# Top-32 attention and MoE on one core: both exponentials of a slot in a row, and the normalising of its weights in the same turn

## The chip, the core and the metric

One NeuronCore of a Trainium2 chip runs the whole program. The metric is the device time of one execution in microseconds (us): the median of three runs. A profiled execution has a time of its own and a span, from its first to its last instruction.

## What is computed

```python
scores = scale * np.matmul(q, k.transpose(0, 1, 3, 2))        # 8 x 8 heads, 576 x 576, head width 64
kth = np.partition(scores, -top_k, axis=-1)[..., -top_k:-top_k + 1]   # top_k = 32
scores = np.where(scores >= kth, scores, -1000000000.0)
attn = np.exp(scores - np.max(scores, axis=-1, keepdims=True))
attn = attn / (np.sum(attn, axis=-1, keepdims=True) + 1e-09)
x = np.matmul(attn, v)              # then reshaped to 4608 tokens x 512
out = ((x @ w1) * (x @ w2) @ w3) @ w_out
```

All is float32. `w3 @ w_out` is formed once at the start.

## The kernel before

The attention is cut into 144 slots, 18 for each of 8 batches: 128 query rows of the two heads of a pair (a = 0, 1), so that a slot's scores are two blocks of 128x576. One **turn** of the loop at L480 (counter `p`) works at four slots at once: it takes the scores of slot i = p+1 out of PSUM, searches the 32 largest of slot p, masks and exponentiates slot j = p-1, and normalises, transposes and multiplies with V slot m = p-2. Who does what:

- **PE** (matmul): scores `st` (L178), nine transposes into `tp` and `ro` (`turn`, L284), 20 products with V into `ro` (`values`, L303), and between them three *fillers* (`fill`, L442) of 11, 11 and 10 matmuls of the MoE of the batch before: 32 a turn. 288 of them make half a batch, so a half takes nine turns.
- **DVE**: the search (`top32_steps`, L212): four max/min over thirds of the row into `w`, then four rounds of MAX8, with match-replace behind the first three. The last MAX8 pair goes over the whole row, 128x576. Also `take_low` (`xf`, reads the values from `ro`), the reciprocal (`invert`, L277), and a product `whole` for the MoE.
- **ACT**: the mask's Relu and the exponentials (`exps`, L270, with a sum over the row as a by-product), the copies out of PSUM (`s` from `st`, `pts` from `tp`, `pr` from `ro`, `xf`), and for the MoE `asb`, `osb` and the cast `g`.
- **POOL** (GpSimd): `edge` (the two bounds of a slot, from its top 32), the mask's subtractions into `pab`, `over`, the addition to the sums (`enlarge`, L274), the two multiplications that normalise `pab` (L280), and for the MoE `g` minus its rounding.

Nothing here is reordered by a scheduler: the class `InOrder` (L37) keeps each engine's instructions in the order in which the Python code issues them, so an engine that waits holds all that stands behind it. All those instructions carry line L49 in the profile, and are told apart by their tiles. In a filler, the evictions that the MoE has put off come first, for example `take_b` (L340): `whole` on DVE, the cast `g` on ACT, the subtraction `g` on POOL.

Buffers that tie the engines: `tp` and the two `st` of a turn share two PSUM buffers (L178, L284: pool `ps_a`), so a turn's `tp` overwrites the first `st` of the turn before, once ACT and DVE have read it. `ro` has one buffer (`ps_v`): its transpose waits for `take_low` of the slot before.

For the first 17 turns or so there is no MoE. In its place `warm` (L465, five times a turn) decodes 40 pieces of the weights in steps on ACT (`t`, `y`), DVE (`z`, `y`) and POOL (`y`, `wo`, `wl`), and PE folds `w3 @ w_out` (`pf`, copied out by ACT and DVE as `wf`).

Of the kernel before, what the change touches and what calls it, by code (L numbers as in the profile page):

```python
# [14 lines left out]
ALU = mybir.AluOpType  # L15
# [42 lines left out]
def attn_moe(ctx: ExitStack, tc: tile.TileContext, q, k, v, w1, w2, w3, w_out, out, flag, general):  # L58
# [12 lines left out]
    pe, act, dve, pool, sp = nc.tensor, nc.scalar, nc.vector, nc.gpsimd, nc.sync  # L71
# [26 lines left out]
    if not general:  # L98
        pe, act, dve, pool, sp = (InOrder(tc, e) for e in (pe, act, dve, pool, sp))
# [78 lines left out]
    def scores(pairs, t):  # L178

        out = []
        for lo, hi in PARTS:
            st = ps_a.tile([128, 2, 512], F32, tag="a", name="st")
            for a in range(2):
                cut = slice(lo + 64, hi + 64) if a == 0 else slice(lo, hi)
                if t == 4:
                    qt, kt, _ = pairs[a]  # L190
                    for i, p in enumerate(HEADS):
                        pe.matmul(st[HEADS[i ^ a], a, : hi - lo], qt[p, 512:], kt[p, cut], start=True, stop=True)
                else:
                    (qt, kt, _), p = pairs[0], HEADS[a]
                    pe.matmul(st[:, a, : hi - lo], qt[p, t * 128 : (t + 1) * 128], kt[p, cut], start=True, stop=True)
            out.append(st)
        return out

    def new_s():
        return att_p.tile([128, 2, S], F32, tag="s", name="s", bufs=3)  # L200
# [5 lines left out]
    def behind(ins, first, why):  # L206
        tc.add_manual_dep(
            ins.ins, first.ins.name, mybir.DependencyInfo(mybir.DependencyClass.Sync, mybir.DependencyReason.DATA),
            reason=why,
        )  # L210

    def top32_steps(s, st, taken, slot):  # L212

        w = att_p.tile([128, 2, S], F32, tag="w", name="w", bufs=1)
        top = tops[slot % len(tops)]  # L220
        one, two, three = slice(0, NG), slice(NG, 2 * NG), slice(2 * NG, S)
        in_two, in_three = st[0][:, :, NG : 2 * NG], st[1][:, :, :NG]
        dve.tensor_tensor(w[:, :, three], s[:, :, one], in_two, op=ALU.max)
        yield dve.tensor_tensor(w[:, :, two], s[:, :, one], in_two, op=ALU.min)
        ins = dve.tensor_tensor(w[:, :, one], w[:, :, three], in_three, op=ALU.max)
        behind(ins, taken, "one engine at a time reads a bank of the scores")
        dve.tensor_tensor(w[:, :, three], w[:, :, three], in_three, op=ALU.min)
        yield
        for i in range(4):
            cut = slice(i * 8, (i + 1) * 8)  # L230
            for a in range(2):
                dve.max(top[:, a, cut], w[:, a, one] if i < 3 else w[:, a, :])
            if i < 3:
                for a in range(2):
                    dve.match_replace(w[:, a, one], top[:, a, cut], w[:, a, one], NEG)
                yield

    def edges_of(slot):
        top = tops[slot % len(tops)]
        edge = small.tile([128, 2, 2], F32, tag="edge", name="edge")  # L240
        pool.tensor_tensor(edge, top[:, :, 0:32:31], coef, op=ALU.mult)
        return edge

    def compare(slot):
        top = tops[slot % len(tops)]
        pool.tensor_tensor(over[:, 2 * slot : 2 * slot + 2], top[:, :, 31], top[:, :, 23], op=ALU.subtract)
# [15 lines left out]
    def new_weights():  # L262
        return att_p.tile([128, 2, S], F32, tag="pab", name="pab"), small.tile([128, 2], F32, tag="sums", name="sums")

    def mask(s, edge, pab, a):

        act.activation(pab[:, a, :], s[:, a, :], AF.Relu, bias=edge[:, a, 1:2], scale=-STEEP)
        pool.tensor_tensor(pab[:, a, :], s[:, a, :], pab[:, a, :], op=ALU.subtract)

    def exps(edge, pab, sums, a):  # L270
        p = pab[:, a, :]
        act.activation(p, p, AF.Exp, bias=edge[:, a, 0:1], scale=SCALE, accum_out=sums[:, a : a + 1])

    def enlarge(sums):  # L274
        pool.tensor_scalar(sums, sums, 1e-9, None, op0=ALU.add)

    def invert(sums):  # L277
        dve.reciprocal(sums, sums)

    def normalise(pab, sums):  # L280
        for a in range(2):
            pool.tensor_scalar(pab[:, a, :], pab[:, a, :], sums[:, a : a + 1], 1.0, op0=ALU.mult, op1=ALU.mult)
# [13 lines left out]
    def take_turned(tp, ro):  # L296
        pts = att_p.tile([128, 2, 512], F32, tag="pts", name="pts", bufs=1)
        act.copy(pts, tp)
        pr = att_p.tile([128, 128], F32, tag="pr", name="pr")
        act.copy(pr, ro[:, :128])  # L300
        return pts, pr
# [21 lines left out]
    def take_high(to, ov):  # L323
        for x, cols, n in to:
            act.copy(x[:, 0, cols], ov[:, n])

    def take_low(to, ov):
        for x, cols, n in to:
            dve.tensor_tensor(x[:, 1, cols], ov[:, n], x[:, 0, cols].bitcast(F32), op=ALU.subtract)
# [69 lines left out]
    if general:  # L399
# [3 lines left out]
        with tc.For_i(0, B, 1) as b:  # L403
            seen = small.tile([1, 1], I32, tag="seen", name="seen", bufs=1)
            nc.sync.dma_start(seen, flag[ds(b + 1, 1), :])
            with tc.If(nc.values_load(seen, min_val=0, max_val=1) > 0):
                kv, xs = {}, {}
                for hps, t in SLOTS:
# [3 lines left out]
                    s, st = new_s(), scores([kv[hp] for hp in hps], t)  # L412
# [20 lines left out]
    kv, ss, sts, edges, pabs, xts, lows = {}, {}, {}, {}, {}, {}, {}  # L433
# [4 lines left out]
    def evict():  # L438
        while put_off:
            put_off.pop(0)()  # L440

    def fill(n):  # L442
        evict()
        while queue and n:
            if next(queue[0], "end") == "end":
                queue.pop(0)
            else:
                n -= 1
# [4 lines left out]
    def fetch_pair(u):  # L453
        if u < B * NHP:
            kv[u] = load_pair(u // NHP, u % NHP)
# [4 lines left out]
    def prefetch(n):  # L460
        while waiting and len(fetched) < n:
            src, step = waiting.pop(0)
            fetched.append((fetch(src), step))

    def warm():  # L465

        if p < 0:
            return
        turns.append(p)
        if fetched and len(turns) % 2:  # L470
            z, step = fetched.pop(0)
            going.append(step(z))
        going[:] = [unit for unit in going if next(unit, "end") != "end"]
        prefetch(3)
# [4 lines left out]
    n_slots = len(slots)  # L479
    for p in range(-1, n_slots + 3):  # L480
        i, j, m = p + 1, p - 1, p - 2
        if i < n_slots and slots[i][1] == 3:
            fetch_pair(slots[i][0][0] + 2)
        finder = top32_steps(ss[p], *sts.pop(p), p) if 0 <= p < n_slots else iter(())
        next(finder, None)
        if 0 <= m < n_slots:
            enlarge(pabs[m][1])
            invert(pabs[m][1])
        if 0 <= j < n_slots:
            edges[j] = edges_of(j)  # L490
        if 0 <= m < n_slots:
            normalise(*pabs[m])
        next(finder, None)
        if m - 1 in lows:
            take_low(*lows.pop(m - 1))
            if m % NS == 0:
                b = m // NS - 1
                queue.append(moe_steps(b, [xts.pop(b * NHP + hp) for hp in range(NHP)], put_off.append))
        warm()
        if 0 <= j < n_slots:  # L500
            pabs[j] = new_weights()
            for a in range(2):
                mask(ss[j], edges[j], pabs[j][0], a)
            compare(j)
        fill(SHARE[0])
        next(finder, None)
        if 0 <= m < n_slots:
            tp, ro = turn(pabs[m][0])
            pts, pr = take_turned(tp, ro)
        warm()  # L510
        if 0 <= j < n_slots:
            exps(edges[j], *pabs[j], 0)
        fill(SHARE[1])
        next(finder, None)
        warm()
        if i < n_slots:
            st = scores(pairs_of(i), slots[i][1])
            ss[i] = new_s()
            take_scores(ss[i], st, 0)
        if 0 <= j < n_slots:  # L520
            exps(edges[j], *pabs[j], 1)
        if i < n_slots:
            sts[i] = st, take_scores(ss[i], st, 1)
        if 0 <= m < n_slots:
            us, t = slots[m]
            for u in us:
                if u not in xts:
                    xts[u] = new_x()
            ov = values([kv[u][2] for u in us], t, pts, pr, ro)
            lows[m] = places([xts[u] for u in us], t), ov  # L530
            take_high(*lows[m])
        next(finder, None)
        warm()
        fill(SHARE[2])
        for _ in finder:
            pass
        if 0 <= m < n_slots:
            del ss[m], pabs[m], edges[m]
        warm()
# [61 lines left out]
```

## Time and profile before

| | |
|---|---|
| time, median of 3 runs | 1324.32 us (1323.19 to 1325.38) |
| profiled execution: its time | 1324.6 us |
| its span | 1322.8 us |
| mean granted TensorE clock | 0.977 |
| busy: PE / DVE / ACT / POOL | 1225.7 / 1144.5 / 949.1 / 863.2 us |

The page gives each engine's busy time as a share of the span. The kernel has three stretches: the start with the decoding (to about 228 us), 126 turns with the MoE of the batch before (to about 1235 us), and the MoE of the last batch, on PE nearly alone. Shares over the whole span mix these, so the stretches are read apart.

### The profile page before, as it was taken

Reading aid. Unit: us, or ns where it says so; the run is one execution under the profiler, and the core shown is the slowest. Engines: PE = TensorE matmul, PEld = TensorE weight load, DVE = VectorE, ACT = ScalarE, POOL = GpSimd, SP = SyncE. Lnnn points to the kernel's source line nnn. Section 1 sums busy time; section 2 is a strip of 40 time slices with the busy share of each in tenths; the row PEclk is TensorE's granted clock in tenths of the full one; section 3 lists DMA queues with packets and bytes.
Section 4 is the critical chain, followed back from the end, with each engine's and each line's share of the span. In section 5 each row is a group of like instructions: output and inputs, shape, how many; then the busy total and the mean of one; then the engine's idle time right before and its main releaser. Section 6 shows DMA issues by size and latency. Waiting matters only on the chain.

```text
span 1322.8 us, 30010 instructions
## 1 busy us (share of the span) xinstructions
PE 1225.7 (93%) x10513; PEld 1045.4 (79%) x10513; DVE 1144.5 (87%) x3980; ACT 949.1 (72%) x2025; POOL 863.2 (65%) x1201
## 2 busy tenths in 40 slices
PE   3688846999999999999999999999999999999996
PEld 1444424888888889888888888888988888888996
DVE  7989889999999999999999999999999999999100
ACT  5776687777777787777777777777777777777311
POOL 4767697776767676766667676767677676667210
PEclk9899877999999999999999999999999999999998
DMA  6343320001020201110010101010111001000000
GB/s 232 115 139 112 126 94 23 28 22 59 17 64 12 68 13 49 31 50 20 27 53 21 59 17 63 13 50 30 49 31 48 22 21 59 17 15 2 19 19 21
DMA packets 28981, 63.89 MB, mean 48 GB/s; under 512 B 3220, under 2 KB 11412, under 8 KB 28820
## 3 DMA queue, kind: packets, MB, share of 16 engines
q1 hardware_dynamic: 28820, 61.88, 14.4%
q8 instruction: 85, 1.39, 0.5%
q14 instruction: 76, 0.62, 0.2%
HBM read 52.43 MB, written 9.44 MB: 47 GB/s over the span
## 4 chain that ended last, share of the span: by engine, by line
PE 75%; POOL 10%; ACT 7%; issue 4%; DVE 3%; DMA 0%; SPq 0%; POOLq 0%; ACTq 0%; DVEq 0%
PE ab L49 26%; PE eo L49 16%; PE st L49 11%; PE ro L49 11%; PE tp L49 9%; POOL pab L49 5%; PE pf L49 3%; ACT pab L49 2%; ACT s L49 2%; POOL g L49 2%; DVE w L49 1%; POOL y L49 1%; DVE top L49 1%; ACT g L49 1%; ACT xf L49 1%
## 5 line engine op out<-in xcount | busy, mean ns | idle before, releaser
L49 DVE MAX8 top<-w 128x8 f32<-128x192 f32 (+1 forms) x1152 | 469.1, 451 | 0.0
L49 PE MATMUL ab<-xf,wh 128*128 128x288 f32 x2048 | 430.6, 300 | 0.0
L49 POOL TENSOR_TENSOR pab<-s,pab 128x576 f32<-128x576 f32 x288 | 404.6, 1429 | 4.7 <-ACT pab L49 4.7
L49 PEld LDWEIGHTS ab<-xf,wh 128*128 128x128 f32 x2048 | 331.3, 189 | 8.3 <-issue 7.4
L49 PE MATMUL ab<-xf,wl 128*128 128x288 f32 x1024 | 307.4, 300 | 0.0
L49 DVE MATCH_REPLACE8 w<-top,w 128x192 f32<-128x192 f32 x864 | 291.2, 347 | 0.0
L49 POOL TENSOR_SCALAR pab<-pab,sums 128x576 f32<-128x576 f32 x288 | 212.5, 753 | 78.4 <-DVE sums L49 57.9
L49 ACT COPY pts<-tp 128x1024 f32<-128x1024 f32 x144 | 146.2, 1015 | 152.7 <-PE tp L49 151.0
L49 ACT ACTIVATE pab<-s,edge 128x576 f32<-128x576 f32 x288 | 209.6, 782 | 54.6 <-POOL edge L49 52.4
L49 PE MATMUL eo<-g,wf 128*128 128x288 f32 x1536 | 228.4, 300 | 0.0
L49 ACT ACTIVATE pab<-pab,edge 128x576 f32<-128x576 f32 x288 | 225.2, 782 | 1.6 <-POOL pab L49 1.3
L49 PE MATMUL tp<-ident,pab 128*128 128x128 f32 x1152 | 166.1, 284 | 64.8 <-POOL pab L49 53.6
L49 ACT COPY s<-st 128x768 f32<-128x768 f32 (+1 forms) x288 | 181.9, 632 | 48.2 <-PE st L49 39.8
L49 PEld LDWEIGHTS eo<-g,wf 128*128 128x128 f32 x1536 | 208.1, 188 | 7.2 <-issue 7.2
L49 PEld LDWEIGHTS tp<-ident,pab 128*128 128x128 f32 x1152 | 134.6, 144 | 88.6 <-POOL pab L49 87.2
L49 PE MATMUL st<-kt,qt 64*128 64x192 f32 (+3 forms) x1280 | 188.8, 445 | 16.0 <-ACT pab L49 7.4
L49 PEld LDWEIGHTS ab<-xf,wl 128*128 128x128 f32 x1024 | 193.6, 189 | 4.8 <-issue 4.8
L49 POOL TENSOR_TENSOR g<-whole,g 128x288 fp32r<-128x288 f32 x128 | 103.0, 805 | 139.7 <-ACT g L49 139.7
L49 DVE TENSOR_TENSOR w<-s,st 128x384 f32<-128x384 f32 x288 | 146.7, 551 | 29.4 <-ACT s L49 18.3
L49 PEld LDWEIGHTS st<-kt,qt 64*128 64x128 f32 (+1 forms) x1280 | 100.2, 182 | 88.9 <-issue 34.8
L49 DVE TENSOR_TENSOR w<-w,st 128x384 f32<-128x384 f32 x288 | 157.7, 548 | 5.0
L49 PE MATMUL ro<-pts,vt 128*64 128x128 f32 (+1 forms) x2560 | 161.5, 269 | 0.0
(46 smaller groups left out, 1128.5 us busy)
## 6 DMA issues: line engine op xcount, KB each, us to landing
z<-in_w SPq DMA_DIRECT2D x32, 512.0 KB, 3.6
vt<-in_v SPq DMA_DIRECT2D x32, 352.0 KB, 3.5
kt<-in_k SPq DMA_DIRECT2D x32, 320.0 KB, 3.3
qt<-in_q SPq DMA_DIRECT2D x32, 288.0 KB, 2.9
out_t<-osb SPq DMA_DIRECT2D x64, 144.0 KB, 1.7
z<-in_wo SPq DMA_DIRECT2D x8, 512.0 KB, 5.0
flag<-missed SPq DMA_DIRECT2D x1, 0.0 KB
seen<-flag SPq DMA_DIRECT2D x1, 0.0 KB
```

The source lines that it names most:

```text
L49: ins = fn(*args, **kw)
```

## The change

The second exponential of slot j is issued directly behind the first, ahead of the two copies of the next scores. The addition to the sums, the reciprocal and the normalising, until now done at the start of the next turn, follow in the same turn: the addition behind `take_high`, the reciprocal and the multiplications behind the third round of the search and ahead of its last MAX8 pair. The first `yield` of the search is gone, as nothing is put in between there now.

```diff
@@ top32_steps
         dve.tensor_tensor(w[:, :, three], s[:, :, one], in_two, op=ALU.max)
-        yield dve.tensor_tensor(w[:, :, two], s[:, :, one], in_two, op=ALU.min)
+        dve.tensor_tensor(w[:, :, two], s[:, :, one], in_two, op=ALU.min)
         ins = dve.tensor_tensor(w[:, :, one], w[:, :, three], in_three, op=ALU.max)
@@ the loop over turns
-        next(finder, None)
-        if 0 <= m < n_slots:
-            enlarge(pabs[m][1])
-            invert(pabs[m][1])
         if 0 <= j < n_slots:
             edges[j] = edges_of(j)
-        if 0 <= m < n_slots:
-            normalise(*pabs[m])
         next(finder, None)
...
             exps(edges[j], *pabs[j], 0)
+            exps(edges[j], *pabs[j], 1)
         fill(SHARE[1])
         next(finder, None)
         warm()
...
             take_scores(ss[i], st, 0)
-        if 0 <= j < n_slots:
-            exps(edges[j], *pabs[j], 1)
-        if i < n_slots:
             sts[i] = st, take_scores(ss[i], st, 1)
...
             take_high(*lows[m])
+        if 0 <= j < n_slots:
+            enlarge(pabs[j][1])
         next(finder, None)
         warm()
+        if 0 <= j < n_slots:
+            invert(pabs[j][1])
+            normalise(*pabs[j])
         fill(SHARE[2])
```

What it moves shows at three places. First ACT, in a turn with the MoE in which a cast `g` comes in the second filler (`pab<-s,edge` is the Relu, `pab,sums<-pab,edge` an exponential, `s<-st` a copy of scores). Before:

```order
L49 ACTIVATE pab<-s,edge 128x576 x2
L49 COPY asb<-ab 128x288
L49 COPY pts<-tp 128x1024
L49 COPY pr<-ro 128x128
L49 ACTIVATE pab,sums<-pab,edge 128x576
L49 CAST g<-whole 128x288
L49 COPY s<-st 128x2x384
L49 ACTIVATE pab,sums<-pab,edge 128x576
L49 COPY s<-st 128x2x192
L49 CAST xf<-ro 128x128
```

and now:

```order
L49 ACTIVATE pab<-s,edge 128x576 x2
L49 COPY asb<-ab 128x288
L49 COPY pts<-tp 128x1024
L49 COPY pr<-ro 128x128
L49 ACTIVATE pab,sums<-pab,edge 128x576 x2
L49 CAST g<-whole 128x288
L49 COPY s<-st 128x2x384
L49 COPY s<-st 128x2x192
L49 CAST xf<-ro 128x128
```

The cast `g` of the second filler now stands behind both exponentials, and the copies of the scores behind all three. Second POOL, over the same turn and the end of the one before, in which `g` came in the first and the third filler (`sums<-sums` is the addition, `pab<-pab,sums` the normalising, `pab<-s,pab` the mask). Before:

```order
L49 TENSOR_TENSOR over<-top_97 128x2
L49 TENSOR_TENSOR g<-whole,g 128x288 x2
L49 TENSOR_SCALAR sums<-sums 128x2
L49 TENSOR_TENSOR edge<-top_95,coef 128x4
L49 TENSOR_SCALAR pab<-pab,sums 128x576 x2
L49 TENSOR_TENSOR pab<-s,pab 128x576 x2
L49 TENSOR_TENSOR over<-top_95 128x2
L49 TENSOR_TENSOR g<-whole,g 128x288
L49 TENSOR_SCALAR sums<-sums 128x2
```

and now:

```order
L49 TENSOR_TENSOR g<-whole,g 128x288
L49 TENSOR_SCALAR sums<-sums 128x2
L49 TENSOR_SCALAR pab<-pab,sums 128x576 x2
L49 TENSOR_TENSOR g<-whole,g 128x288
L49 TENSOR_TENSOR edge<-top_95,coef 128x4
L49 TENSOR_TENSOR pab<-s,pab 128x576 x2
L49 TENSOR_TENSOR over<-top_95 128x2
L49 TENSOR_TENSOR g<-whole,g 128x288
L49 TENSOR_SCALAR sums<-sums 128x2
L49 TENSOR_SCALAR pab<-pab,sums 128x576 x2
```

Before, the `g` of the third filler stood ahead of the addition to the sums; now it stands behind the normalising and ahead of the next `edge`, and it is the `g` of the second filler that stands between a slot's mask and the addition to the same slot's sums. Third ACT at the start, in a turn with decoding (`t<-z` and `y<-z` are decoding steps). Before:

```order
L49 COPY pr<-ro 128x128
L49 ACTIVATE t<-z 128x512
L49 ACTIVATE y<-z 128x512
L49 ACTIVATE pab,sums<-pab,edge 128x576
L49 COPY s<-st 128x2x384
L49 ACTIVATE pab,sums<-pab,edge 128x576
L49 COPY s<-st 128x2x192
L49 CAST xf<-ro 128x128
L49 ACTIVATE t<-z 128x512
```

and now:

```order
L49 COPY pr<-ro 128x128
L49 ACTIVATE t<-z 128x512
L49 ACTIVATE y<-z 128x512
L49 ACTIVATE pab,sums<-pab,edge 128x576 x2
L49 COPY s<-st 128x2x384
L49 COPY s<-st 128x2x192
L49 CAST xf<-ro 128x128
L49 ACTIVATE t<-z 128x512
```

The second exponential no longer stands between a copy that waits for PE's scores and the decoding step behind it.

## Rows read from the trace of the kernel before

**Rows 1.** Stretches: length, busy us (instructions) of PE PEld DVE ACT POOL, PEclk, DMA
```profile
14.00:228.00 214.00, 144.95 (x837) 83.27 (x838) 191.34 (x580) 152.88 (x301) 157.34 (x185) 0.88 0.33 109
309.00:453.00 144.00, 142.90 (x1300) 126.24 (x1298) 135.68 (x487) 110.90 (x242) 99.10 (x142) 1.00 0.12 37
```

**Rows 2.** Waits, 309 to 453 us: who on whom, us in total, times, longest
```profile
DVE sums L49 <- POOL sums L49: 3.3, 4, 0.9
```

**Rows 3.** Timeline of DVE, one turn without MoE work, and a start nine turns later
```profile
717.75 1.02 DVE L49 TENSOR_TENSOR w<-s,st 128x384 f32<-128x384 f32 x2
...
719.80 0.28 DVE L49 TENSOR_TENSOR xf<-ro,xf 128x128 fp32r<-128x128 f32 x1
...
723.51 1.42 DVE L49 MAX8 top<-w 128x8 f32<-128x576 f32 x2
725.03 0.56 DVE L49 TENSOR_TENSOR w<-s,st 128x384 f32<-128x384 f32 x1
...
789.82 0.55 DVE L49 TENSOR_TENSOR w<-s,st 128x384 f32<-128x384 f32 x1
```

**Rows 4.** Timeline of PE: the transposes of two turns in a row
```profile
784.64 1.03 PE L49 MATMUL tp<-ident,pab 128*128 128x128 f32 x8
...
792.49 0.38 PE L49 MATMUL tp<-ident,pab 128*128 128x128 f32 x2
```

**Rows 5.** Timeline of a turn behind a third-filler g: POOL, DVE, ACT
```profile
749.93 0.80 POOL L49 TENSOR_TENSOR g<-whole,g 128x288 fp32r<-128x288 f32 x1 [3.01 <-ACT g L49]
750.80 0.21 POOL L49 TENSOR_SCALAR sums<-sums 128x2 f32<-128x2 f32 x1
751.10 0.20 POOL L49 TENSOR_TENSOR edge<-top,coef 128x4 f32<-128x4 f32 x1
751.31 1.47 POOL L49 TENSOR_SCALAR pab<-pab,sums 128x576 f32<-128x576 f32 x2
752.75 2.81 POOL L49 TENSOR_TENSOR pab<-s,pab 128x576 f32<-128x576 f32 x2
...
751.05 0.17 DVE L49 RECIPROCAL sums<-sums 128x2 f32<-128x2 f32 x1 [0.81 <-POOL sums L49]
...
753.57 0.45 DVE L49 TENSOR_TENSOR whole<-ab,asb 128x288 f32<-128x288 f32 x1
753.93 0.61 DVE L49 MAX8 top<-w 128x8 f32<-128x192 f32 x2
...
751.33 1.44 ACT L49 ACTIVATE pab<-s,edge 128x576 f32<-128x576 f32 x2 [1.47 <-POOL edge L49]
...
753.59 1.02 ACT L49 COPY pts<-tp 128x1024 f32<-128x1024 f32 x1 [0.54 <-PE tp L49]
...
754.65 0.79 ACT L49 ACTIVATE pab<-pab,edge 128x576 f32<-128x576 f32 x1
...
755.42 0.43 ACT L49 CAST g<-whole 128x288 fp32r<-128x288 f32 x1
...
755.93 0.80 POOL L49 TENSOR_TENSOR g<-whole,g 128x288 fp32r<-128x288 f32 x1 [0.22 <-ACT g L49]
```

**Rows 6.** Waits of DVE at the start, 14 to 228 us
```profile
DVE z L49 <- ACT y L49: 14.4, 14, 3.0
DVE wf L49 <- ACT wf L49: 3.5, 2, 2.5
```

**Rows 7.** Timeline of one turn at the start
```profile
136.28 1.01 DVE L49 TENSOR_TENSOR w<-s,st 128x384 f32<-128x384 f32 x2
...
138.27 1.97 PE L49 MATMUL tp<-ident,pab 128*128 128x128 f32 x8 [3.70 <-POOL pab L49]
...
146.38 0.80 ACT L49 COPY s<-st 128x768 f32<-128x768 f32 x1 [2.99 <-PE st L49]
147.07 0.78 ACT L49 ACTIVATE pab<-pab,edge 128x576 f32<-128x576 f32 x1
...
149.63 0.69 DVE L49 TENSOR_SCALAR z<-t 128x512 int32<-128x512 int32 x1 [3.05 <-ACT y L49]
```

## The prediction, before the changed kernel was run

> **What bounds the kernel now.** I read the stretches first, then the waits, then single turns of the timeline. Of the profiled execution's 1324.6 us (0.3 above the median of 1324.32), the start and the 126 turns with MoE work matter here; the MoE of the last batch runs behind the last turn and has nothing to do with the exponentials. In the turns with MoE PE is busy 142.9 of 144 us and DVE 135.7 of 144 [rows 1]: two engines within a few per cent of full, so neither share says what a wait is worth. The timeline does. Nine turns, half a batch of MoE, take 789.82 - 717.75 = 72.07 us on DVE [rows 3]. PE, where nothing holds it, repeats its turn in 792.49 - 784.64 = 7.85 us [rows 4], nine times 70.65. So 1.42 us of every nine turns are lost to waits of PE; there are fourteen such nines, and **20 us is all that these turns can give**. DVE alone would need 725.03 - 717.75 = 7.28 us for a turn without MoE work [rows 3], and 0.36 more for each `whole` (753.57 to the next start at 753.93) [rows 5]; a nine has eight of them, so DVE has little more room than PE while the `g` come.
>
> Where the 1.42 goes is seen in rows 5. A `g` of the third filler is cast late on ACT, behind the copies of the scores, and its subtraction stands on POOL ahead of the addition to the sums (749.93, 750.80); the reciprocal waits 0.81 for that, the normalising starts only at 751.31, and the transposes behind it. That happens in two turns of nine: four waits, 3.3 us in a batch [rows 2].
>
> **The change, part by part, in the turns with MoE.** No instruction is added or dropped; the reciprocal's 0.08 (its share of DVE's pipelined issue) only moves. No DMA moves, and neither SP's nor POOL's queue is passed by one. What moves are waits.
>
> *Gone*: the normalising (1.44, from 751.31 to 752.75) no longer stands between a slot's bounds and its mask on POOL [rows 5], and a third-filler `g` no longer stands ahead of the sums. The transposes no longer wait for the normalising, which now ends in the turn before.
>
> *What is late next*: two things. First the reciprocal, now ahead of the last MAX8 pair. I count from the start of DVE's turn. DVE comes to it at 723.51 - 717.75 - 0.08 = 5.68, or 6.04 with a `whole` before it, and the next turn starts 1.60 after it (0.08, and 1.52 from 723.51 to 725.03) [rows 3]; 1.96 with a third-filler `whole`. Second the transpose into `ro`, which must wait for `take_low`: that ends at 719.80 + 0.28 - 717.75 - 0.08 = 2.25 [rows 3]. With some 0.15 for the signal and the weight load, and 0.9 from the first transpose to that one, **the transposes count as starting at 1.50 at the earliest**.
>
> Call x the place in DVE's turn at which PE starts the transposes. Next turn's x is x + 7.85 minus DVE's turn; where this falls below 1.50, PE loses the difference. The second exponential starts at the later of two times. By way of PE: transposes 1.03 and 0.1 of signal [rows 4], 1.06 from `pts` to the first exponential, 0.77 from that to the next ACT instruction [rows 5], so x + 2.96. By way of POOL, behind a third-filler `g`: from the last reciprocal 0.26 to the normalising, 1.44 for it, 0.87 for `g` (749.93 to 750.80), 0.23 from `edge` to the Relu, about 0.85 to the mask (half of 1.44, and a signal), 2.82 for the mask [rows 5]: 6.47, less the 1.96 of the turn's end, so 4.51. From its start to the reciprocal: 1.21 without a `g` (0.96 until the sum is there, an estimate from 0.77 and the 0.2 that the sum's read adds; 0.25 from addition to reciprocal). With a second-filler `g` in between: 0.77, 0.51 from cast to subtraction, 0.87, 0.25: **2.40** [rows 5].
>
> Now the nine turns. In the three without `g` DVE waits for the exponential, harmlessly: the turn ends 2.96 + 1.21 + 1.60 = 5.77 after the transposes, x settles at about 2.07. Turn 1 (`g` in first and third filler): 8.21 long, x 1.71. Turn 2 (second filler): the exponential at 4.67, the reciprocal at 7.07, 1.0 late; 8.67 long, x 0.89: **0.61 lost**. Turn 3 (first filler; its cast stands ahead of `pts`, the reciprocal comes at about 6.16): 7.76 long, x 1.59. Turn 4 (first and third): 8.12, x 1.32: **0.18 lost**. Turn 5 (second): exponential at 4.51, reciprocal at 6.91, 8.51 long, x 0.84: **0.66 lost**. Turn 6: 7.76. Sum 1.45, against 1.42 now: the wait moves from the `g` of the third filler to that of the second. Fourteen times 0.03, with something for a slot that has two `take_low`: **plus 1 us**. The bounds are minus 20 (no wait left) and, with 0.3 more lost in each of the three places, plus 13; I take the sum, as all but two of its parts are rows.
>
> **The start.** Here DVE is busy 191 of 214 us [rows 1], and waits 14.4 us for decoding steps of ACT and 3.5 for `wf` [rows 6]. The long ones have one form, in four turns: PE's transposes wait 3.70 for the normalising, the fold and the scores follow late, ACT waits 2.99 for the scores, then runs the second exponential and the second copy before the decoding that DVE waits 3.05 for [rows 7]. The exponential leaves that place: 0.78. The transposes start 1.99 into the turn (138.27 - 136.28); they can now start at about 1.1, when the search has read the old scores: 0.9 earlier. So 1.7 each in the three waits of 2.5 and over, and the 1.0 that is left of the 3.5 [rows 6]: 6. Of some dozen shorter waits I take 2 back in all: in part of them the exponential now stands ahead of the decoding instead. **Minus 8**; at most minus 19, at worst plus 3, if only that (0.77, four times) counted.
>
> First the row, then a rule: after its wait of 3.70 PE takes 1.97 for eight transposes [rows 7] that take 1.03 in the full stretch [rows 4], and the granted clock of the start is 0.88 of full speed [rows 1]. The Trainium skill, "TensorE: Matmul & The Clock Gate", Part 1, says that an idle TensorE falls to half clock and that work brings it back. By that rule shorter waits could also give back 0.94 in each of about seven turns, 6.6 us more; my sum leaves it out, since 2.8 of a wait of 3.7 would remain.
>
> Together: 1324.6 - 8 + 1 = **1317.6 us**.
>
> **The rivals.**
> *Both waits go* (0.13). If the second-filler `g` reaches POOL while DVE is still in its third round, nothing replaces the 1.42: 1317.6 - 21 = 1297. For it: the mask starts 1.44 earlier. Against: cast and subtraction stand behind the second exponential in program order, and 4.67 + 2.40 is past 6.04 by a whole microsecond.
> *Slower: first-filler turns lose too* (0.22). There the cast stands ahead of `pts`, and both exponentials now stand behind `pts` and ahead of the reciprocal, where before the second had until the next turn. The point is 7.85 - 1.60 = 6.25 for the reciprocal, 0.09 past my 6.16. If it comes at 6.55 (a `whole` that waits 0.3 for `asb`, say), four turns of nine lose 0.30 each, 17 us in fourteen nines, less what the second-filler turns then no longer lose in x, about 5: 1330.
> *The start gives nothing* (0.20), because DVE's decoding waits only change their releaser: 1324.6 + 1, and the execution stays where it is, 1325.
> *That the change does not take place* can be ruled out: the order of the instructions shows it on ACT, POOL and DVE.
>
> **How the numbers follow.** My case, 0.45: 1317.6, itself from 1312 to 1323. A measurement of this kernel tells about 0.2%, 2.6 us, from no change. Faster: my case all but an edge of 0.03, and both waits gone, 0.55. Within 0.2%: three quarters of "the start gives nothing" and that edge, 0.18. Slower: 0.27. The range takes in the slower rival whole and stops short of the fastest: 1302 to 1332.
>
> **What would show it.** In the turns with MoE: the wait of the reciprocal for the sums grows from 3.3 us a batch to about 7, in second-filler turns and in those without `g`; DVE's wait for the scores' copies goes; the transposes wait for DVE, not POOL; nine turns take 72.1. At the start: the waits of 3.05 fall to about 1.4 and the MoE begins some 8 us sooner. I am wrong if nine turns take under 71.5 or over 72.8, or if the start is not shorter by 3 us at least.

## The result, and the profile after

The changed kernel takes 1310.38 us (median of 4 runs, 1309.74 to 1310.61) against 1323.76 (4 runs, 1322.28 to 1325.38): a ratio of 0.9898, 95% interval 0.9881 to 0.9915, 13.4 us faster. The forecast was 1317.6, faster by 6.7: the direction held and the time lies in the range, but the gain is twice the forecast's.

In the profiled execution (1309.74 us, span 1308.0) the time goes at two places. The first turn in which DVE has MoE work starts here, in the kernel before and then in the changed one (timeline of DVE):

```profile
237.06 0.55 DVE L49 TENSOR_TENSOR w<-s,st 128x384 f32<-128x384 f32 x1
```
```profile
225.76 0.56 DVE L49 TENSOR_TENSOR w<-s,st 128x384 f32<-128x384 f32 x1
```

So the start is 11.3 us shorter (forecast 8). From there to the last turn but one the distance shrank by 2.6 (forecast: 1 longer). The rest, 1.0, lies behind it. The 11.3 is a difference of two executions, and such starts scatter: with the old order there, another execution (the second experiment's) has 235.36; with the new one, two others have 226.24 and 224.95.

The stretches that answer to [rows 1], with the same columns:

```profile
14.00:228.00 214.00, 153.65 (x940) 91.84 (x941) 201.69 (x614) 163.08 (x320) 165.06 (x197) 0.90 0.34 111
309.00:453.00 144.00, 143.32 (x1303) 126.63 (x1302) 136.21 (x488) 110.39 (x241) 99.47 (x143) 1.00 0.12 37
```

At the start DVE now works 201.69 of 214 us, ten more than before, since the stretch now takes in 614 of its instructions instead of 580; in the turns with MoE hardly anything shows in the shares. The waits show more. At the start, against [rows 6] (DVE at 14 to 228 us; who on whom, us in total, times, longest):

```profile
DVE z L49 <- ACT y L49: 7.5, 9, 1.8
DVE sums L49 <- POOL sums L49: 1.4, 3, 0.7
```

The waits for decoding halve, 14.4 to 7.5, and those of 3.5 for `wf` are gone; the reciprocal's own wait (`sums`) stays at 1.4 (1.5 before). In the turns with MoE, against [rows 2]:

```profile
DVE sums L49 <- POOL sums L49: 5.0, 8, 0.9
```

That is more than the 3.3 of before, though the turns are shorter: the wait has moved. The turn below has a `g` of the second filler; it answers to [rows 5] (timeline of ACT, POOL, DVE; in brackets the idle time ahead and what ended it):

```profile
310.35 0.77 ACT L49 ACTIVATE pab<-pab,edge 128x576 f32<-128x576 f32 x1
...
311.11 0.42 ACT L49 CAST g<-whole 128x288 fp32r<-128x288 f32 x1
...
311.61 0.80 POOL L49 TENSOR_TENSOR g<-whole,g 128x288 fp32r<-128x288 f32 x1 [1.35 <-ACT g L49]
...
312.48 0.21 POOL L49 TENSOR_SCALAR sums<-sums 128x2 f32<-128x2 f32 x1
...
312.73 0.17 DVE L49 RECIPROCAL sums<-sums 128x2 f32<-128x2 f32 x1 [0.86 <-POOL sums L49]
```

From exponential to reciprocal 2.38 us pass (2.40 in the prediction), and DVE stands 0.86 for a `g` that has nothing to do with the sums. Nine turns, against [rows 3]:

```profile
297.46 0.55 DVE L49 TENSOR_TENSOR w<-s,st 128x384 f32<-128x384 f32 x1
...
369.34 0.55 DVE L49 TENSOR_TENSOR w<-s,st 128x384 f32<-128x384 f32 x1
```

71.88 us, where PE alone would need 70.65: 1.23 are still lost. Last the turn of [rows 7] at the start, which fell from 14.69 to 11.33 us:

```profile
130.22 1.00 DVE L49 TENSOR_TENSOR w<-s,st 128x384 f32<-128x384 f32 x2
...
131.38 1.07 PE L49 MATMUL tp<-ident,pab 128*128 128x128 f32 x8 [2.98 <-POOL edge L49]
...
135.71 0.76 ACT L49 ACTIVATE pab<-pab,edge 128x576 f32<-128x576 f32 x1
...
137.20 1.18 ACT L49 COPY s<-st 128x768 f32<-128x768 f32 x2 [0.63 <-PE st L49]
...
140.22 0.69 DVE L49 TENSOR_SCALAR z<-t 128x512 int32<-128x512 int32 x1 [0.17 <-ACT y L49]
```

The transposes start 1.16 into the turn, not 1.99; the second exponential runs before the scores are there; DVE's wait of 3.05 is 0.17. Two of these gains were forecast. The third was not put into the sum: the eight transposes take 1.07 us behind a wait of 2.98, where they took 1.97 behind one of 3.70. And this turn is the best case: in two other executions with the same order at the start the fold behind the transposes ran slowly (5.22 and 5.10 us, against 3.60 here), and the turn took 12.98 and 12.91. The long turn like it, turn 5 (turns count from 0; this is turn 11), took 13.01 here, with a wait of 1.85 for decoding.

### The profile page after: what moved, and what is told of

Its sections match the earlier page's. It is cut to its first block, busy times and chain, and to the rows that moved or that the text cites. A ratio compares the mean times of both kernels' runs of the same rounds, so it can differ in the third digit from the quotient of the medians.

```text
span 1308.0 us, 29999 instructions
## 1 busy us (share of the span) xinstructions
PE 1222.7 (93%) x10513; PEld 1043.8 (80%) x10513; DVE 1144.5 (88%) x3980; ACT 943.6 (72%) x2025; POOL 863.3 (66%) x1201
## 4 chain that ended last, share of the span: by engine, by line
PE 69%; DVE 12%; ACT 10%; POOL 4%; issue 4%; DMA 0%; DVEq 0%; ACTq 0%; SPq 0%; POOLq 0%
PE ab L49 24%; PE eo L49 15%; PE ro L49 11%; PE st L49 9%; PE tp L49 7%; DVE w L49 5%; DVE top L49 4%; ACT pab L49 4%; PE pf L49 3%; ACT pts L49 3%; POOL g L49 2%; POOL pab L49 1%; DVE y L49 1%; DVE z L49 1%; DVE xf L49 1%
## 5 line engine op out<-in xcount | busy, mean ns | idle before, releaser
L49 ACT ACTIVATE pab<-pab,edge 128x576 f32<-128x576 f32 x288 | 222.0, 779 | 1.7 <-POOL pab L49 1.5
L49 PE MATMUL tp<-ident,pab 128*128 128x128 f32 x1152 | 155.5, 279 | 51.2 <-DVE w L49 35.0
L49 ACT COPY s<-st 128x768 f32<-128x768 f32 (+1 forms) x288 | 170.2, 648 | 8.9 <-PE st L49 8.9
```

The costliest lines, as they stand in the source:

```text
L49: ins = fn(*args, **kw)
```

## The experiments

The theory after this reading: most of the gain is at the start, where order and PE's clock both have a part, and what the turns with MoE still lose hangs on the second filler's `g`.

**Where the gain lies.** Two kernels have the new order in one part of the program alone:

```diff
+    def new_exp(p):
+        return p < 20          # the other kernel: p >= 20
...
+            if new_exp(p):
+                exps(edges[j], *pabs[j], 1)
...
+        if 0 <= j < n_slots and not new_exp(p):
+            exps(edges[j], *pabs[j], 1)
```

and a second switch, `new_norm`, likewise for sums, reciprocal and normalising. New order at the start alone:

> The new order in the 20 turns of the start, the old order in all turns after. Theory (most of the gain comes from the start; in the traces its last turn before the MoE begins 11.3 us sooner, and the turns with MoE give 2.6): the start shortens by 11 again, the nine turns stay at 72.07, so about 1323.8 - 11 = 1312.5. Rival (part of the shift at the start is handed back or borrowed by the turns with MoE, and the start is worth my forecast 8 alone): 1316. Rival (the turns made the gain): 1321 or more.

Measured: 1313.76 (0.9922, 0.9908 to 0.9936), 10.5 less than 1324.31. New order in the turns alone:

> The old order in the 20 turns of the start, the new order after. Theory: 2.6 of gain in the turns with MoE, nine turns at 71.88, 1321. By my forecast's working (1.45 lost per nine where 1.42 was lost): 1324 to 1325. If it is under 1317, the start was not the main place.

Measured: 1321.22 (0.9978, 0.9969 to 0.9987), 3.1 less, and nine turns in 71.86 us. The parts add up to 13.6, the whole was 13.4: within the scatter neither part lends from the other.

**What the turns still lose.** The addition moves ahead of the second filler:

```diff
             exps(edges[j], *pabs[j], 1)
+            if p >= 20:
+                enlarge(pabs[j][1])
         fill(SHARE[1])
...
-        if 0 <= j < n_slots:
+        if 0 <= j < n_slots and p < 20:
             enlarge(pabs[j][1])
```

> The changed kernel, and in the turns with MoE the addition to the sums stands on POOL directly behind the mask, ahead of the second filler's g. Theory (what PE still loses, about 1.2 us per nine turns, hangs on that g, which holds the sums and so the reciprocal for 0.86 and 0.73): both waits go, nine turns take 70.7 to 71.0, and 14 nines give 12 to 16, so 1295 to 1298. Rival (the transpose into ro, which waits for take_low, bounds the turn anyway): only the part of the loss that the late reciprocal made goes, nine turns at 71.4, about 1304. Rival (g, now later, holds the normalising or the next slot's mask as long as it held the sums): 1308 to 1312.

Measured: 1293.35 (0.9766, 0.9753 to 0.978), 17 less than the changed kernel. A second-filler turn of it, POOL and DVE:

```profile
309.27 0.21 POOL L49 TENSOR_SCALAR sums<-sums 128x2 f32<-128x2 f32 x1 [1.06 <-ACT pab L49]
...
309.58 0.80 POOL L49 TENSOR_TENSOR g<-whole,g 128x288 fp32r<-128x288 f32 x1
309.75 0.15 DVE L49 RECIPROCAL sums<-sums 128x2 f32<-128x2 f32 x1
```

The reciprocal no longer waits, and `g` behind it holds nothing that shows. Nine turns go from here to here:

```profile
295.43 1.02 DVE L49 TENSOR_TENSOR w<-s,st 128x384 f32<-128x384 f32 x2
...
366.12 1.02 DVE L49 TENSOR_TENSOR w<-s,st 128x384 f32<-128x384 f32 x2
```

70.69 us, PE's own 70.65: the whole loss is gone, so the transpose into `ro`, which waits for `take_low`, was no limit beside it.

**Which half of the change it is.** First the second exponential alone, directly behind the first, with sums, reciprocal and normalising at the start of the next turn as before; then these alone, with the exponential behind the first copy of the scores as before. The cut is shown against the kernel with the new order at the start alone:

```diff
     def new_exp(p):
-        return p < 20
+        return True            # the second kernel: False
     def new_norm(p):
-        return p < 20
+        return False           # the second kernel: True
```

> The kernel before, with the second exponential directly behind the first, ahead of the scores' copies; addition, reciprocal and normalising stay at the start of the next turn. Theory (the start's gain has two parts, the exponential out of the way of the scores' copies and the decoding, and the transposes that no longer wait for the normalising; only the second shortens PE's waits and so keeps its clock up): 0.8 in each of four long turns, minus 3, and nothing in the turns with MoE, where the third filler's g still stands ahead of the sums: 1321. Rival (the exponential alone makes the start's gain): 1313. Rival (the copies, now later, hold the next scores): 1325 or more.

Measured: 1322.49 (0.9989, 0.998 to 0.9998), 2.0 less; the total is near the theory's, the places are not. The first turn with MoE starts later than before (238.74, against 237.06 and 235.36 in the two executions with the old order), and nine turns take 71.78 instead of 72.07, worth 4:

```profile
309.97 0.55 DVE L49 TENSOR_TENSOR w<-s,st 128x384 f32<-128x384 f32 x1 [0.36 <-ACT s L49]
...
381.75 0.56 DVE L49 TENSOR_TENSOR w<-s,st 128x384 f32<-128x384 f32 x1 [0.36 <-ACT s L49]
```

The theory is wrong in both. DVE at the start shows why:

```profile
DVE z L49 <- ACT y L49: 20.1, 17, 2.9
```

14.4 before, 7.5 in the changed kernel. With the normalising still ahead of the mask on POOL, the exponential comes late, and where it used to stand behind the decoding it now stands ahead of it. So in turn 8, which took 10.68 us before and takes 12.07 here (ACT, then DVE):

```profile
106.92 0.77 ACT L49 ACTIVATE pab<-pab,edge 128x576 f32<-128x576 f32 x1 [0.51 <-POOL pab L49]
...
108.20 0.62 ACT L49 ACTIVATE t<-z 128x512 f32<-128x512 f32 x1
108.76 0.66 ACT L49 ACTIVATE y<-z 128x512 int32<-128x512 uint16 x1
...
109.46 0.69 DVE L49 TENSOR_SCALAR z<-t 128x512 int32<-128x512 int32 x1 [1.46 <-ACT y L49]
```

> Addition, reciprocal and normalising in the same turn, ahead of the last search, as in the changed kernel, but the second exponential still behind the first copy of the scores. Theory (the two moves need each other: in the turns with MoE the second exponential then waits for the scores, so the reciprocal stands 0.8 to 1.1 later than in the changed kernel, past the point where x falls under 1.50 in every turn, 0.5 to 1 lost in each of nine; at the start DVE's reciprocal waits for scores that come 6 to 9 us into the turn): nine turns 75 to 77, 1370 to 1400. Rival (DVE has the room): within 10 of the changed kernel, 1310 to 1320.

Measured: 1398.54 (1.0561, 1.0545 to 1.0577), 5.6% slower, as the theory had it. One turn of it with MoE work but without `g`:

```profile
308.63 1.24 PE L49 MATMUL st<-kt,qt 64*128 64x384 f32 x8
...
309.59 0.80 ACT L49 COPY s<-st 128x768 f32<-128x768 f32 x1 [0.74 <-PE st L49]
...
310.29 0.78 ACT L49 ACTIVATE pab<-pab,edge 128x576 f32<-128x576 f32 x1
...
311.25 0.21 POOL L49 TENSOR_SCALAR sums<-sums 128x2 f32<-128x2 f32 x1 [2.50 <-ACT pab L49]
...
311.49 0.17 DVE L49 RECIPROCAL sums<-sums 128x2 f32<-128x2 f32 x1 [1.12 <-POOL sums L49]
```

The chain scores, copy, exponential, sums, reciprocal closes into a loop of 8.50 us, and nine turns take 77.63 (313.08 to 390.71). At the start this half has its first MoE turn at 235.13, no clear gain on 237.06 and 235.36. Neither half shortens the start beyond the scatter, both together take some 11 off it: **at the start the two moves work only together**. In the turns with MoE this is not so: there the exponential alone (71.78) does as well as both (71.88).

**PE's clock.** Twelve idle transposes (of the identity, into columns that nothing reads) at the end of a turn keep PE at work in the wait that follows:

```diff
+        if 0 <= m < 17:          # the other kernel: m in (2, 7, 8)
+            for _ in range(12):
+                pe.transpose(ro[:, 256:384], ident, ident)
```

In all turns of the start of the kernel before:

> The kernel before, with 12 extra 128x128 transposes of the identity at the end of each turn of the start, into columns of ro that nothing reads; they only keep PE at work (about 1.6 us at the upper clock) in the wait ahead of the turn's transposes. Theory (a part of the start's 11.3 is PE's clock: before, the transposes of turns 5 and 11 took 1.97 behind waits of 3.7 and more, after, 1.06 behind waits of 3.0): those transposes take 1.06, the fold behind them is faster too, and the kernel gains 2 to 4 us, 1320 to 1322, with no change of order. Rival (the clock is a bystander; the start gained because the exponential and the normalising left their places): 1323.8 or up to 3 more, for the extra transposes stand ahead of folds that would have started.

Measured: 1320.40 (0.997, 0.9958 to 0.9982), 3.9 less. In three turns:

> The kernel before, with the 12 idle transposes in three turns alone: at the end of turns 4, 9 and 10, ahead of turns 5, 10 and 11, which they shortened by 2.3, 1.4 and 2.3 when they stood in every turn, while turns 4, 7 and 13, whose folds stood behind them, grew by 1.0, 1.2 and 0.6. Theory (the clock is worth about 6 us of the start before): 1318. Rival (the turns that grew were late because the others were early): 1320.4 as with all.

Measured: 1319.70 (0.9967, 0.9955 to 0.9979), 4.8 less, between theory and rival. Turn 11 of the kernel before, then of this one (stretches over transposes and fold; the third number from the end is PEclk):

```profile
138.20:140.20 2.00, 1.93 (x9) 1.93 (x10) 1.97 (x6) 0.39 (x1) 2.00 (x4) 0.50 0.00 0
140.20:145.40 5.20, 5.20 (x10) 1.97 (x8) 4.78 (x20) 3.06 (x6) 5.20 (x5) 0.68 0.34 102
```
```profile
136.10:137.40 1.30, 1.19 (x9) 0.96 (x10) 1.26 (x4) 0.38 (x1) 1.30 (x2) 1.00 0.42 166
137.40:141.00 3.60, 3.60 (x13) 1.41 (x10) 3.57 (x15) 3.08 (x6) 3.60 (x5) 1.00 0.42 146
```

Before, the transposes ran wholly at the lower level (0.50, 1.2 GHz) and the fold partly (0.68); with the idle work both run at 2.4 GHz. Turns 5, 10 and 11 are 2.31, 1.37 and 2.28 shorter, 5.96 together, without any change of order. Turns 6 and 7 grew by 1.7: there a fold that had run at full clock now ran slowly (timeline of PE, before and with the idle work in three turns):

```profile
79.78 3.70 PE L49 MATMUL pf<-wo,y 128*128 128x512 f32 x8 [0.47 <-POOL y L49]
```
```profile
77.27 5.40 PE L49 MATMUL pf<-wo,y 128*128 128x512 f32 x8 [0.48 <-POOL y L49]
```

With idle work in every turn, turns 4, 7 and 13 cost 1.0, 1.2 and 0.6: their transposes start 4.04, 4.40 and 4.28 into the turn, where they had started 1.99, 3.07 and 2.97.

**Both together.** The kernel with the early addition, and the idle transposes ahead of turns 5, 9 and 11:

> The kernel with the sums ahead of the second filler's g (1293.35), and 12 idle transposes at the end of three turns of the start, ahead of turns 5, 9 and 11, where PE waits 2.4 to 3.0 for its transposes and the fold behind them still runs slowly in some executions (scores 7.5 to 7.7 into the turn, 6.0 where the fold runs at full clock). Theory (the clock still costs 1.5 in two of these three turns): minus 2 to 4, 1290. Rival (DVE, busy over 9 tenths of the start, is the bound by now, and the slow folds cost it nothing): 1293.

Measured: 1290.38 (0.9746, 0.9733 to 0.976), 3.0 less than with the early addition alone, and all of it at the start, where the first MoE turn comes at 221.83 instead of 224.95 (DVE, early addition alone, then with the idle work):

```profile
224.95 0.55 DVE L49 TENSOR_TENSOR w<-s,st 128x384 f32<-128x384 f32 x1
```
```profile
221.83 0.56 DVE L49 TENSOR_TENSOR w<-s,st 128x384 f32<-128x384 f32 x1
```

This is the fastest kernel here, 34 us ahead of the one before (1324.49 in the same comparison) and 20 ahead of the changed one. Its edit, beside that of the early addition, is the loop above with `m in (2, 6, 8)`.

## What the prediction had right, and which of its terms failed

The direction held, but two terms of the sum did not, and both erred the same way. The turns, put at plus 1, gave 2.6 back: the step that failed is "the reciprocal comes at about 6.16". The start, put at minus 8, gave 10.5 to 11.3: there the clock was left out at nothing, and it was worth 1 to 3. That the time still lies in the range owes to the range's width, 1302 to 1332, not to the sum.

*The start, minus 8.* Place, direction and mechanism held: [rows 7]'s chain is gone, the exponential out of the copies' way, the transposes earlier. Two sizes failed. The clock term, "my sum leaves it out, since 2.8 of a wait of 3.7 would remain", should have been in: such a wait remained (2.98) and the transposes took 1.07 all the same. Not all of that is the clock: with the idle work, in the old order and at granted clock 1.00, the same eight take 1.38.

```profile
136.14 1.38 PE L49 MATMUL tp<-ident,pab 128*128 128x128 f32 x8 [1.54 <-POOL pab L49]
```

The larger price of the lower level is in the fold, 5.24 against 3.60 us, which the prediction left unpriced. Compared at full clock in these long turns, the kernel before would start its MoE at 237.06 - 5.96 = 231.1, and the new order starts it at 221.8 with the idle work. So about 9 us come from the order. The changed kernel still loses 3.3 to the clock in this execution (turns 5 and 9 take 13.01 and 13.53, with the idle work 11.33 and 11.88), where the kernel before lost 6. So the clock gave back 1 to 3: 2.7 by these turns, 1.5 if the start's gain is taken as the 10.5 that the new order at the start alone gave. These are sums over executions whose starts differ by up to 1.7 us, not single measurements. The Trainium skill, "TensorE: Matmul & The Clock Gate", Part 1, has PE fall to half clock in idle time and come back with work; the granted clocks of 0.50 and 1.00 above agree. The other size is "of some dozen shorter waits I take 2 back in all": at full clock (the idle work on both sides) turns 9 and 11 are each 1.1 shorter, and turn 4, where neither kernel needs it, 1.4 (11.76 to 10.33). That is less for each turn than the 1.7 of the long waits, but in more turns than I counted; turns 6 and 12 give back 1.1 each.

*The turns, plus 1.* Nearly every step of the working is there. The wait moved to the second filler's `g`; the reciprocal came at 7.02 and 6.96 into those turns (7.07 and 6.91 forecast), the turns were 8.61 and 8.54 long (8.67 and 8.51). The transposes' limit of 1.50 held too: behind such a turn they start at 1.16, and the weight load of the one into `ro` waits 0.33 for `take_low`, 1.50 in effect. The step that failed is "the reciprocal comes at about 6.16" in turn 3, behind a first-filler cast, a figure for which the prediction shows no working. This is that turn of the changed kernel (DVE and PE's weight load):

```profile
314.32 1.02 DVE L49 TENSOR_TENSOR w<-s,st 128x384 f32<-128x384 f32 x2
...
316.64 0.14 PEld L49 LDWEIGHTS ro<-ident,pab 128*128 128x128 f32 x1 [0.33 <-DVE xf L49]
...
320.39 0.15 DVE L49 RECIPROCAL sums<-sums 128x2 f32<-128x2 f32 x1
...
321.97 1.02 DVE L49 TENSOR_TENSOR w<-s,st 128x384 f32<-128x384 f32 x2
```

The reciprocal came at 6.07 with no wait; the turn took 7.65, not 7.76, x stayed 0.1 higher, and the fourth turn (8.02, not 8.12) lost none of its 0.18. 1.23 lost in nine instead of 1.45, against 1.42 before: fourteen times 0.19 is the 2.6, and the allowance for "a slot that has two `take_low`" does not show. Of the signs named, DVE's wait for the scores' copies is gone from the waits, and the reciprocal's grew, to 5.0 instead of some 7.

*The rivals.* "Both waits go" was a true ceiling, and the experiment with the early addition reaches it in these turns; the change did not, for the reason given. "First-filler turns lose too" had the sign of the error wrong: the reciprocal came earlier than taken, 0.18 ahead of the point (6.07 against 6.25), and the half of the change without the exponential shows what lies behind that point: 5.6% slower. "The start gives nothing" is refuted by the new order at the start alone.

## What to carry to other kernels

When a reduction's last small step shares an in-order queue with filler work, put it directly behind its producer: here the place of one 0.21 us addition was worth 17 us, more than the change itself. Two moves that each free the other's input must be costed together, and by stage: alone one of them gave 0.1% and the other cost 5.6%, and at the start neither had the gain of both. Where PE waits a few microseconds again and again, read the granted clock of what follows the wait, and price the work behind it at both levels.

## What the runs showed of the hardware

The half clock doesn't always meet the work directly behind a wait. In turn 5 of the changed kernel the transposes behind a wait of 2.99 ran at full clock, and only the fold behind them ran slowly; in turn 11, behind 2.98, neither did. Stretches over transposes and fold of turn 5, then of turn 11:

```profile
60.00:61.20 1.20, 1.06 (x8) 0.86 (x8) 1.17 (x4) 1.14 (x2) 1.20 (x2) 1.00 0.05 14
61.40:66.60 5.20, 5.20 (x10) 1.90 (x9) 5.13 (x19) 3.80 (x9) 4.57 (x6) 0.67 0.30 102
131.30:132.40 1.10, 1.02 (x8) 0.86 (x8) 1.07 (x3) 1.00 (x2) 1.10 (x2) 1.00 1.01 377
132.70:136.20 3.50, 3.50 (x9) 1.34 (x8) 3.47 (x15) 3.50 (x8) 3.50 (x4) 1.00 0.74 264
```

Turn 5 took 13.01 us, turn 11 11.33, with the same order of work. In the kernel with the early addition, whose order at the start is the same, it was the other way round: turn 5 took 11.33 and turn 11 12.91, with its transposes, then its fold, like this:

```profile
129.40:130.50 1.10, 1.05 (x8) 0.81 (x8) 1.06 (x4) 1.09 (x2) 1.10 (x1) 0.97 0.93 249
130.80:135.90 5.10, 5.10 (x11) 1.99 (x10) 5.03 (x18) 3.76 (x9) 4.47 (x6) 0.70 0.60 209
```

So which turn has the slow fold changes between executions of one order, and a single turn's gain is no measure of a change. And kept away from one turn, the slow stretch can come in a later one, as in turn 6 with the idle work in three turns, whose granted clock over the turn was 0.85 where it had been 1.00. Why it falls there and not elsewhere was not tried. The twelve idle transposes held the clock in turns 5, 10 and 11. With idle work in every turn they did not in turns 14 and 16: a wait of 3.46 and 3.51 remained behind them, and the eight transposes took 1.97 again.
